# One more four-slot tile with seven-product pairs, a new written order, and early queries loaded in 2 KB runs

## The chip, the cores and the metric

The kernel runs on one core of a Trainium2 chip. TensorE (PE) does the matmuls, VectorE (DVE), ScalarE (ACT) and GpSimd (POOL) the elementwise work, and SyncE (SP) issues most DMAs. The metric is device time in microseconds; a lower one is better. Three runs of the kernel before gave 218.16, 218.23 and 218.40 us. The profiled execution that all rows come from has a span of 216.57 us from its first to its last instruction.

## The reference

Inputs are q, k and v of 4 batches, 8 heads, 768 tokens and 64 values a head, and three weights. First a retention with a decay per head, written as a recurrence:

```
state = gamma[h] * state + outer(k[t], v[t])
y[t]  = (1 / 8) * q[t] @ state
```

Then y, 3072 tokens by 512, goes through a bilinear feed-forward block of width 1536: `out = ((x @ w_a) * (x @ w_b)) @ w_out`. Outputs are float32; the kernel multiplies in bf16 and adds in float32.

## The kernel before

The 3072 tokens are 24 **slots** of 128, six to a batch. The recurrence is done in slots: q and k are scaled by powers of the decay (`scaled`, L281), so that within a slot the attention is a masked product of scores (`scores`, L366) with the values (`intra`, L415), and across slots a state of 64 x 64 a head is carried (`update`, L381) and multiplied by q (`inter`, L403). `leave` (L424) copies the finished y, transposed, to bf16 as the feed-forward input xt. Before that, q and k must be turned: `flip` (L330) does it with a transposing DMA on SP's queue.

Batch 0 is special, since nothing else can run until it is there. Its slots are handled in three pairs: one DMA loads 256 tokens of k, q or v with 2 tokens x 64 values (512 B) in a run (`load_two`, L135), partition p holding tokens 2p and 2p+1. `casts2` (L459) scales, `flip2` (L469) transposes on PE, and `scores2`, `update2`, `inter2`, `intra2` and `leave2` (L481 to L536) do the rest. The exponents for the scaling are made on the chip by `tables` (L196): an iota on POOL, a product on DVE, an exponential on ACT; the masks are memsets and selects on POOL (L219, L222), and `late_tables` (L229) makes a second set of tables for the other batches. `warm` (L549) puts idle matmuls on PE while it waits.

The slots are grouped in **tiles** for the feed-forward block: `TILES = [4, 2, 2, 2, 2, 4, 8]` (L16). The two stages of the block are tiled differently:

- First stage. For a plain tile, `ffn_a` (L560) and `ffn_g` (L574) multiply one block of 128 of the 1536 columns of w_a and of w_b with the whole tile as moving operand (256 or 512 columns, four matmuls each). ACT copies the first product to bf16, DVE multiplies the second with it. There are 12 such blocks. The tile of eight slots and, in part, the last tile of four (slots 12 to 15) use Strassen's scheme in Winograd's form instead: seven products of half size for eight, from sums of weight blocks (`weight_piece`, L807) and sums of inputs (`x_sum`, L827; `xf_sum`). For the eight-slot tile these are the classes `Unit` (L840, moving operand 512 columns); for the four-slot tile `Quad` (moving operand 256), for two pairs of blocks, p = 0 and 1, each pair and each weight on its own.
- Second stage. For all tiles but the first, a `Group` (L663) of seven products of 6 matmuls x 256 columns makes the outputs of two slots, from sums of the first stage (`hsum`, L642) and of w_out (`weight_sum`, L622). The first tile uses plain products (`ffn_out`, L599).

The order of work on every engine is the order of the program's text: `seq` chains each instruction to the one ahead of it on its engine. Up to the last block of tile 0 the text is a straight list. Behind it, calls such as `blocks(3, 6, 7)`, `turn(12, 10)` (L434: update, scores of the new pair, inter, intra and copy of the old pair, in one block), `hsums` and `casts(14)` stand in an order written by hand, with three strings for the laced stretches (`START`, `END`, `LACED`). `casts` also issues the loads of later slots. PE's accumulators are eight banks: three in a ring ("ff"), two for scores, two for y, one for the state.

Of the kernel before, what the change touches and what calls it, by code (L numbers as in the profile page):

```python
# [15 lines left out]
TILES = [4, 2, 2, 2, 2, 4, 8]  # L16
# [3 lines left out]
START = ("A1 A2 u0.1 u1.1 A6 T X3 A7 B1 X2 A5 B6 B7 X1 A3 B5 u0.2 u1.2 B2 X4 A4 u0.6 B3 u1.6 B4 u0.5 u1.5 "  # L20
         "u0.7 u2.1 u0.3 u1.7 u2.6 u1.3 u0.4 u2.2 u3.1 u2.5 u1.4 u2.7 u3.6")
END = ("u11.1 u10.5 u10.7 u9.4 u11.6 u10.3 u11.2 S03 a1< u11.5 u11.7 u10.4 b1< u11.3 a1> b1> c1< d1< u11.4 a7 c1> d1> c2 d2 "
       "S02 S01 b7 a2 b2 S04 a6 b6 S13 a5 b5 S12 a3 b3 a4 b4 S11 c7 d7 c6 d6 S14 c5 d5 "
       "c3 c4 d4 d3")
V_LATE = range(12, 20)
LACED = ("X3 X2 m1 m7 m2 a1 b1 a2 b2 m6 X1 a6 b6 a7 b7 F2 X4 m5 a5 b5 K20 G2 a3 b3 a4 b4 V18 "
         "m3 c1 d1 F3 H3 c2 d2 c6 d6 c7 d7 c5 d5 m4 c3 d3 V19 c4 d4 G3")
# [4 lines left out]
def kernel(  # L32
# [78 lines left out]

    def raw_tile(shape, dtype, tag, name):
        return raw.tile(shape, dtype, tag=tag, name=name, bufs=3 if tag == "vf" else 2)
# [3 lines left out]
    def load_slot(t, names="kqv"):  # L117
        b, ci = divmod(t, NCH)
        for nm in names:
            src = {"k": k, "q": q, "v": v}[nm]  # L120
            if nm == "q":
                if t % 2 == 0:
                    load_two(nm, src, b, ci // 2, t)
                continue
            if t % 2 == 0:
                whole[nm] = raw_tile([P, 2, H, D], F32, nm + "f", nm + "f")
            raws[nm, t] = whole[nm][:, t % 2]
            s = src[b, :, ci * P : (ci + 1) * P, :].rearrange("h p d -> p h d")
            seq(nc.sync.dma_start(out=raws[nm, t], in_=s))

    def load_slots(t):
        for u, names in ((t, "kq"), (t + 1, "k"), (t, "v"), (t + 1, "v")):
            load_slot(u, names)
# [8 lines left out]
    def load_pair(u):  # L142
        for nm, src in (("k", k), ("q", q), ("v", v)):
            load_two(nm, src, 0, u, 2 * u)
# [25 lines left out]
    def issue_loads(n):  # L170
        for _ in range(min(n, len(pending))):
            what = pending.pop(0)
            n = int(what[1:])
            if what[0] in "ab":
                load_wide(what[0], n)
            elif what[0] in "kqv":
                load_two(what[0], {"k": k, "q": q, "v": v}[what[0]], 0, n, 2 * n)
            else:
                {"p": load_pair, "s": load_slots, "t": load_slot, "w": load_w, "o": load_o}[what[0]](n)


    kqb = {}
# [11 lines left out]
    tabs = []  # L194

    def tables(pattern, channel):  # L196
# [8 lines left out]
        if not tabs:  # L205
            qtab = const.tile([P, NCH, H, 1], F32, name="qtab")
            seq(nc.scalar.activation(qtab[:, :, :, 0], earg, AF.Exp, bias=bq))
            tabs.append(qtab)
        tabs.append(ktab)

    tables([[2 * P, PAIRS], [1, 2], [0, 1]], 2)
    make_identity(nc, ident)
# [4 lines left out]
    for par in range(2):  # L217
        m = const.tile([P, 1, P], BF16, name=f"mask{par}")
        seq(nc.gpsimd.memset(m, 1.0))  # L219
        for c in range(2):  # L220
            mc = m[64 * c : 64 * c + 64]
            seq(nc.gpsimd.affine_select(out=mc, in_=mc, compare_op=ALU.is_ge, fill=0.0,  # L222
                                        base=-par, pattern=[[0, 1], [1, 2], [2, 64]],
# [5 lines left out]
    def late_tables():  # L229
# [3 lines left out]
        tables([[P, NCH], [0, 1]], 1)  # L233

# [32 lines left out]
    def cast_o(j):  # L267
        cast(nc.gpsimd, wo_bf[:, j * FPO : (j + 1) * FPO, :], wst["o", j])
# [12 lines left out]
    def scaled(eng, t, i):  # L281
        tab = tabs[0] if i else tabs[1 if t < 2 * PAIRS else 2]
# [5 lines left out]
        else:  # L288
            dst = dst.rearrange("p hp r d -> p r hp d")
# [3 lines left out]

    def new_nat(t):
        kqb[t] = nat.tile([P, 2, HP, 2, D], BF16, tag="kqb", name="kqb")
        kb[t], qb[t] = kqb[t][:, 0], kqb[t][:, 1]
        vb[t] = nat.tile([P, H, D], BF16, tag="vb", name="vb")

    def casts(t, between=lambda: None):
        new_nat(t)  # L300
        scaled(nc.gpsimd, t, 0)
        between()
        scaled(nc.gpsimd, t, 1)
        if t not in range(12, 20):
            cast(nc.gpsimd, vb[t], raws["v", t])
        u = t + 2
        if u == 20:
            load_slot(u, "kq")
        flip(t)
        if u == 20:  # L310
            load_slot(u + 1, "k")
            return
        if u == 21:
            load_slot(u - 1, "v")
            load_slot(u, "v")
            load_slot(22, "kq")
            return
        if u in V_LATE:
            if u == 13:
                load_slot(12, "q")  # L320
            elif u == 19:
                load_slot(18, "kq")
            load_slot(u, {12: "k", 18: ""}.get(u, "kq"))
            if u % 2:
                load_slot(u - 1, "v")
                load_slot(u, "v")
        elif u < NSLOT:
            load_slot(u)

    def flip(t):  # L330
        if t % 2 == 0:
# [4 lines left out]

    def late_kq(t):
        for u in (t, t + 1):
            new_nat(u)
            scaled(nc.gpsimd, u, 0)  # L340
            scaled(nc.gpsimd, u, 1)
            flip(u)
        if t == 20:
            load_slot(23, "k")
            load_slot(22, "v")
            load_slot(23, "v")

    def casts_two(t):
        for u in (t, t + 1):
            new_nat(u)  # L350
# [52 lines left out]
    def inter(t):  # L403
        if t % NCH == 0:
            return
# [863 lines left out]
```

## Time and profile before

| | |
|---|---|
| median of three runs | 218.23 us |
| profiled execution, span | 216.57 us |
| granted TensorE clock, mean | 1.000 |
| ACT busy | 104.9 us |
| POOL busy | 154.2 us |
| DVE busy | 147.5 us |
| DMA | 39.68 MB, 85162 packets |

A row of the timeline view reads: start, time until the last of the merged instructions ends, engine, line, operation, what is written from what, the part of PE's array in use (rows by columns), partitions by elements and type, how often; in brackets the idle time of the engine just before, and what ended it. Several equal instructions in sequence are merged into one row, and matmuls are pipelined, so the next row can start ahead of the end of the one before. In the windows view each engine has its busy time and its count, and the last three numbers are the granted clock, the DMA share and GB/s. DMA rows give the packets, their sizes and the mean rate of a stretch.

### The profile page before, as it was taken

To read this page: it belongs to the slowest core of one execution; us is meant where nothing else is said; L and a number is where in the kernel's file an instruction comes from. 1 tells how busy PE (TensorE), PEld (TensorE's weight loads), DVE (VectorE), ACT (ScalarE), POOL (GpSimd) and SP (SyncE) were. 2 spreads that over 40 slices of the span, in tenths; PEclk is the share of its full clock that TensorE was granted. 3 is DMA by queue.
4 is the path that set the end of the run, shared out by engine and by line. 5 is a ranking of instruction groups with operands and counts; after the bars stand their busy time and mean duration, and the time that the engine had idled before them with its cause. 6 is when DMAs were issued, how large, how long until landed. Compare 5 with 4: busy or idle time off the path is not lost.

```text
span 216.6 us, 5713 instructions
## 1 busy us (share of the span) xinstructions
PE 210.7 (97%) x2252; PEld 146.1 (67%) x2252; DVE 147.5 (68%) x272; ACT 104.9 (48%) x235; POOL 154.2 (71%) x184
## 2 busy tenths in 40 slices
PE   7889999999999999999999999999999999999994
PEld 3557445587458888888888877457864444458883
DVE  3777346845984486356377978676577987688962
ACT  3256325343224444464576475657546656652331
POOL 5265876879878678969869979899986999530000
PEclk9999999999999999999999999999999999999999
DMA  5999999999999999999979999950013000000055
GB/s 162 290 320 365 387 311 360 384 268 232 221 264 227 228 231 222 158 192 269 197 169 245 222 209 234 236 127 3 5 69 125 2 0 3 2 0 0 27 194 170
DMA packets 85162, 39.68 MB, mean 183 GB/s; under 512 B 57488, under 2 KB 78864, under 8 KB 85136
## 3 DMA queue, kind: packets, MB, share of 16 engines
q1 hardware_dynamic: 84992, 39.26, 76.8%
q8 instruction: 17, 0.28, 0.5%
q14 instruction: 9, 0.07, 0.1%
q10 hardware_dynamic: 144, 0.07, 0.1%
HBM read 28.31 MB, written 6.29 MB: 160 GB/s over the span
## 4 chain that ended last, share of the span: by engine, by line
PE 91%; SPq 3%; DMA 3%; POOL 0%; issue 0%; DVE 0%
PE a L568 18%; PE g L580 18%; PE mA L685 12%; PE uA L859 10%; PE mB L685 6%; PE o L605 5%; PE uB L859 5%; SPq L138 3%; DMA wsta<-in_moe_w_a_dram 3%; PE mC L685 3%; PE at L372 2%; PE uC L859 2%; PE y L420 2%; PE st L390 2%; PE fa L949 2%; PE fb L949 1%
## 5 line engine op out<-in xcount | busy, mean ns | idle before, releaser
L582 DVE TENSOR_TENSOR ht<-g,asb 128x256 bf16<-128x256 f32 (+1 forms) x70 | 34.4, 493 | 31.6 <-PE g L580 28.0
L568 PE MATMUL a<-xt,wa_bf 128*128 128x256 bf16 (+1 forms) x280 | 48.6, 300 | 0.1
L580 PE MATMUL g<-xt,wb_bf 128*128 128x256 bf16 (+1 forms) x280 | 48.4, 300 | 0.0
L571 ACT CAST asb<-a 128x256 bf16<-128x256 f32 (+1 forms) x70 | 30.0, 429 | 33.3 <-PE a L568 31.1
L580 PEld LDWEIGHTS <-wb_bf 128*128 128x128 bf16 x280 | 27.0, 98 | 10.2 <-POOL wb_bf L251 0.2
L568 PEld LDWEIGHTS <-wa_bf 128*128 128x128 bf16 x280 | 26.5, 98 | 10.7 <-POOL wa_bf L251 0.4
L292 POOL TENSOR_TENSOR kqb<-kf,ktab 128x512 bf16<-128x512 f32 x22 | 23.6, 1078 | 7.4 <-DMA kf<-in_k_dram 4.9
L866 ACT COPY snap<-uA 128x512 f32<-128x512 f32 x36 | 20.0, 588 | 15.4 <-PE uA L859 13.9
L685 PEld LDWEIGHTS <-hs 128*128 128x128 bf16 x234 | 22.8, 98 | 3.6
L378 DVE TENSOR_TENSOR aT<-at,mask 128x512 bf16<-128x512 f32 x36 | 22.3, 682 | 0.3
L292 POOL TENSOR_TENSOR kqb<-qf,qtab 128x512 bf16<-128x512 f32 x18 | 19.6, 1088 | 2.7 <-DMA qf<-in_q_dram 2.7
L618 POOL TENSOR_TENSOR ht<-gsb,asb 128x512 bf16<-128x512 bf16 x13 | 15.2, 1175 | 7.5 <-DVE gsb L618 7.4
L692 ACT COPY snaps<-mA 128x256 f32<-128x256 f32 x30 | 11.0, 374 | 18.9 <-PE mA L685 18.9
L685 PEld LDWEIGHTS <-ht 128*128 128x128 bf16 x180 | 17.5, 98 | 3.3
L618 POOL TENSOR_TENSOR hs<-ht 128x384 bf16<-128x384 bf16 (+3 forms) x14 | 15.9, 1134 | 3.5 <-DVE ht L582 3.5
L618 POOL TENSOR_TENSOR hs<-ht,hs 128x384 bf16<-128x384 bf16 (+1 forms) x17 | 16.9, 997 | 1.5 <-DVE ht L582 1.4
L685 PE MATMUL mA<-wsum,hs 128*128 128x256 bf16 x120 | 15.2, 273 | 0.0
L618 DVE TENSOR_TENSOR osb<-mB,snaps 128x256 f32<-128x256 f32 x20 | 8.4, 421 | 8.3 <-ACT snaps L692 4.4
L251 POOL CAST vb<-vf 128x512 bf16<-128x512 f32 x12 | 7.5, 641 | 6.7 <-DMA vf<-in_v_dram 6.7
L605 PE MATMUL o<-wo_bf,ht 128*128 128x512 bf16 x48 | 10.7, 379 | 0.0
L618 DVE TENSOR_TENSOR asb<-uB,snap 128x512 bf16<-128x512 f32 x12 | 8.2, 685 | 3.1 <-ACT snap L866 2.0
L618 DVE TENSOR_TENSOR gsb<-uB,snap 128x512 bf16<-128x512 f32 x12 | 8.2, 686 | 2.9 <-ACT snap L866 2.1
(138 smaller groups left out, 374.7 us busy)
## 6 DMA issues: line engine op xcount, KB each, us to landing
qf<-in_q_dram SPq DMA_DIRECT2D x12, 512.0 KB, 6.1
out_dram<-osb SPq DMA_DIRECT2D x21, 256.0 KB, 4.1
kf<-in_k_dram SPq DMA_DIRECT2D x18, 256.0 KB, 5.1
vf<-in_v_dram SPq DMA_DIRECT2D x18, 256.0 KB, 5.3
wsta<-in_moe_w_a_dram SPq DMA_DIRECT2D x6, 512.0 KB, 7.7
wsto<-in_moe_w_out_dram SPq DMA_DIRECT2D x6, 512.0 KB, 8.7
wstb<-in_moe_w_b_dram SPq DMA_DIRECT2D x5, 512.0 KB, 8.3
kf<-in_k_dram SPq DMA_DIRECT2D x3, 512.0 KB, 7.1
```

The costliest lines, as they stand in the source:

```text
L292: seq(eng.tensor_tensor(dst, src, tab, op=ALU.mult))
L378: seq(nc.vector.tensor_tensor(aT[t][:, r], at[r], mask.to_broadcast([P, HP, P]), op=ALU.mult))
L568: seq(nc.tensor.matmul(a, wa_bf[:, kt, fs], xcols(J, kt, c0, c1), start=(kt == 0), stop=(kt == KT - 1)))
L571: seq(nc.scalar.copy(asb, a))
L580: seq(nc.tensor.matmul(g, wb_bf[:, kt, fs], xcols(J, kt, c0, c1), start=(kt == 0), stop=(kt == KT - 1)))
L582: seq(nc.vector.tensor_tensor(ht[J][:, ft, c0:c1], g, asbs.pop((J, ft, c0)), op=ALU.mult))
L605: seq(nc.tensor.matmul(o, ht[J][:, ft, i * P : (i + 1) * P], wo_bf[:, ft], start=(ft == 0), stop=(ft == NFT - 1), skip_group_check=True))
L618: seq(eng.tensor_tensor(dst, x, y, op=op))
L685: seq(nc.tensor.matmul(m, w, right[:, j], start=(first and j == 0), stop=(j == NP - 1), skip_group_check=True))
L692: seq(nc.scalar.copy(self.snaps[:, n], self.bank["A"]))
L859: seq(nc.tensor.matmul(m, w, right[:, k], start=(first and k == 0), stop=(k == 1), skip_group_check=True))
L866: seq(nc.scalar.copy(self.snaps[n], self.bank["A"]))
```

## The change

Three things are changed.

1. `TILES` becomes `[4, 2, 2, 4, 4, 8]`: slots 8 to 11 are one tile. Both middle four-slot tiles (now numbers 3 and 4) use seven products for eight in the pairs p = 0 and 1. A class `Duo` replaces `Quad`: it takes both weights of a pair together, w_a in the left half of a bank and w_b in the right half, so that one ACT copy or one DVE sum treats 512 columns and the product of the two halves follows from that.
2. The hand-written calls and strings are replaced by one string `ORDER` of small steps, each with its engine where there is a choice (D, G and A for DVE, POOL and ACT). `turn` is gone: updates (U), scores (S), inter (I), intra (N) and copies (L) are steps of their own. Scalings of k and q (k, y), value casts (v), casts of w_out (C), sums (h, w, W, x, X), loads (l), flips (f) and stores (s) are steps too. On ACT a scaling is eight instructions, one a head.
3. For batch 0, q is loaded by two DMAs a pair, in runs of 8 tokens x 64 values (2 KB). A partition then holds one group of 8 tokens of one pair of heads. The queries come out of the transposition in another order, so `scores2` and `inter2` read them with a step of four values (`queries2`), masks and `leave2` follow that order, and a table of its own (`qtab2`) with the position and decay of each partition is made at the start. The usual q table is made later, in `late_tables`.

```
-TILES = [4, 2, 2, 2, 2, 4, 8]
+TILES = [4, 2, 2, 4, 4, 8]
+DUO = {3: {0: ('F', 'b', 'F', 'DGG', 'KKT'), 1: ('F', 'Z', 'F', 'DGG', 'OTO')}, 4: {0: ('F', 'b', 'F', 'DGG', 'KKT'), 1: ('F', 'Z', 'F', 'DGG', 'OTO')}}
+ORDER = """
+a.1.0 w.a.3.0.2.G C.4.G s w.a.2.0.2.D s C.3.G a.1.1 C.0.G C.2.G s a.1.2 w.b.3.0.2.D g.1.1 s C.5.G g.1.0 s
...
+w.b.2.0.2.D s a.1.5 g.1.10 g.1.4 g.1.9 g.1.5 s v.6.G y.6.G k.6.A s a.1.11 g.1.8 y.7.A f.6 k.8.G f.7
+g.1.11 s o.0.0 l.k.9 s W.3.D o.2.0 o.2.1 U.6.D l.v.9 o.0.1 l.k.10 W.2.D y.8.G f.8 W.1.D W.4.D l.v.10
+o.1.0 S.6.at.2 s S.7.y.2 v.7.G s o.1.1 h.1.3.0.6.D o.3.0 k.9.A h.1.2.0.6.D l.q.10 s v.10.G s o.3.1
...
+a.2.11 g.2.11 h.2.2.3.6.G h.2.1.3.6.G y.13.G h.2.4.3.6.G M.2.0.1 l.k.15 M.2.0.7 x.3.3.D y.14.G d.3.0.1
+x.3.2.D v.12.G d.3.0.7 x.3.1.D f.13 s M.2.0.6 d.3.0.2 M.2.0.2 d.3.0.6 d.3.1.1 a.3.2 x.3.4.D M.2.0.5
...
+    def load_pair_q(u):
+        f = raw_tile([P, 2, 8 * D], F32, "qf", "qf")
+        s = q[0, :, 2 * u * P : 2 * (u + 1) * P, :].rearrange("(hp r) (n j) d -> r n hp (j d)", r=2, j=8)
+        for r in range(2):
+            seq(nc.sync.dma_start(out=f[:, r], in_=s[r]))
...
     tables([[2 * P, PAIRS], [1, 2], [0, 1]], 2)
+    pick = osbp.tile([P, 3, HP, 32], F32, tag="osb", name="pick")
+    seq(nc.vector.tensor_copy(pick[:, :2], lgr.rearrange("p o (i r) -> p r i o", r=2).to_broadcast([P, 2, HP, 32])))
+    seq(nc.gpsimd.iota(pick[:, 2], pattern=[[0, HP], [8, 32]], base=0, channel_multiplier=0,
+                       allow_small_or_imprecise_dtypes=True))
+    posq = const.tile([P, PAIRS, 1, 8], F32, name="posq")
+    seq(nc.gpsimd.iota(posq, pattern=[[2 * P, PAIRS], [0, 1], [1, 8]], base=-MID,
+                       channel_multiplier=0, allow_small_or_imprecise_dtypes=True))
+    seq(nc.gpsimd.affine_select(out=pick, in_=pick, compare_op=ALU.is_equal, fill=0.0, base=0,
+                                pattern=[[0, 3], [-1, HP], [-4, 32]], channel_multiplier=1))
+    lgp = const.tile([P, 1, 3, 1], F32, name="lgp")
+    seq(nc.vector.tensor_reduce(lgp[:, 0, :, 0], pick.rearrange("p a i n -> p a (i n)"),
+                                axis=mybir.AxisListType.X, op=ALU.add))
...
+    seq(nc.scalar.activation(qtab2[:, :, :, :, 0], argq, AF.Exp, bias=bq))
     make_identity(nc, ident)
...
+            if eng is nc.scalar:
+                for h in range(H):
+                    seq(nc.scalar.mul(dst[:, h % HP, h // HP, :], src[:, h, :], tab[:, h, :]))
+                return
...
+    def queries2(u, rows, hp, c):
+        cols = kqT2[u].rearrange("p a b c (n i) -> p a b c i n", i=HP)
+        return cols[rows, :, 1, :, hp, 16 * c : 16 * c + 16]
...
-                                         kqT2[u][half(r), :, 1, hp, half(c)],
+                                         queries2(u, half(r), hp, c),
...
-            cast(eng, xt[J][:, i : i + 2, :, half(c)],
-                 ys[u][c].rearrange("p k (two n) -> p two k n", two=2))
+            cast(eng, xt[J][:, i + c].rearrange("p k (n j) -> p k n j", j=8),
+                 ys[u][c].rearrange("p k (j n) -> p k n j", j=8))
```

In `ORDER`, a and g are the two products of a plain block (tile, block), d a step of a `Duo` (tile, pair, product), M a step of a `Group` (tile, group, product), u a step of a `Unit`, o half of a plain output.

More of the change, by code (lines that the diff above doesn't have):

```diff
@@ L415, in intra @@
     def intra(t):
+        need(("S", t), ("v", t))
+        done.add(("N", t))
+        y_banks(t)
         for r in range(2):
@@ L575, in ffn_g @@
         c1 = TILES[J] * P if c1 is None else c1
+        done.update(("h", J, ft, c) for c in range(2))
         fs = slice(ft * P, (ft + 1) * P)
@@ L1242 @@
+    for step in ORDER.split():
+        kind, *args = step.split(".")
+        STEPS[kind](*args)
 _INS = ['q', 'k', 'v', 'moe_w_a', 'moe_w_b', 'moe_w_out']
```

675 lines of the change are left out of this document (295 added, 380 removed).

## The prediction

> **What bounds the kernel now.** The front page comes first, for who is busy; then the windows view in two stretches, cut where the first four-slot tile is through its feed-forward block; then PE's timeline, to see whether a busy PE is ever kept waiting.
>
> ```profile
> span 216.6 us, 5713 instructions
> PE 210.7 (97%) x2252; PEld 146.1 (67%) x2252; DVE 147.5 (68%) x272; ACT 104.9 (48%) x235; POOL 154.2 (71%) x184
> ```
>
> ```profile
> 0.00:42.00 42.00, 39.23 (x450) 22.32 (x450) 26.11 (x54) 17.89 (x35) 26.57 (x50) 1.00 1.05 320
> 42.00:216.60 174.60, 171.47 (x1803) 123.78 (x1802) 121.39 (x219) 87.01 (x200) 127.61 (x135) 1.00 0.71 150
> ```
>
> PE is busy for 171.47 us of the last 174.60, at clock 1.00, and no other engine reaches 75% there. Busy is not yet full speed, so the price of one matmul is read from starts:
>
> ```profile
> 42.51 0.60 PE L580 MATMUL g<-xt,wb_bf 128*128 128x256 bf16 x4
> 43.05 0.60 PE L568 MATMUL a<-xt,wa_bf 128*128 128x256 bf16 x4
> ...
> 112.06 0.60 PE L580 MATMUL g<-xt,wb_bf 128*128 128x256 bf16 x4
> 112.49 0.60 PE L568 MATMUL a<-xt,wa_bf 128*128 128x256 bf16 x4
> 113.01 0.60 PE L580 MATMUL g<-xt,wb_bf 128*128 128x256 bf16 x4
> 113.56 0.60 PE L568 MATMUL a<-xt,wa_bf 128*128 128x256 bf16 x4
> ...
> 138.20 1.03 PE L568 MATMUL a<-xt,wa_bf 128*128 128x512 bf16 x4
> 139.06 1.03 PE L580 MATMUL g<-xt,wb_bf 128*128 128x512 bf16 x4
> ```
>
> From 112.06 to 112.49 four matmuls of 256 columns take 0.436 us, 0.109 each; from 138.20 to 139.06 four of 512 take 0.864, 0.216 each. A step longer than that is a wait. Between feed-forward matmuls behind 42 us I find only four above 0.05 us, the first at 43.05 (0.11 over), the last at 113.56 (0.11 over), 0.38 together. So the kernel is PE's own list of matmuls, behind a start that ends near 18 us and ahead of a short tail.
>
> One thing in the list is not columns:
>
> ```profile
> 56.76 3.83 PE L605 MATMUL o<-wo_bf,ht 128*128 128x512 bf16 x17
> 60.52 0.32 PE L390 MATMUL st<-vb,kqb 128*64 128x64 bf16 x8
> ...
> 150.78 0.71 PE L685 MATMUL mA<-wsum,hs 128*128 128x256 bf16 x5
> 151.42 0.42 PE L410 MATMUL y<-kqT,gst 64*64 64x128 bf16 x16
> 151.77 0.64 PE L420 MATMUL y<-aT,vb 128*64 128x128 bf16 x16
> 152.34 0.83 PE L685 MATMUL mB<-wsum,hs 128*128 128x256 bf16 x6
> ```
>
> The number pair ahead of the tile size is the part of the array in use. When it changes, about 0.095 us pass: 17 x 0.216 = 3.67 from 56.76, and the next start is 0.09 later; 5 x 0.109 = 0.545 from 150.78, and the next is 0.095 later. Behind 42 us I count 39 such changes, the first at 60.52, the last at 152.34.
>
> **Columns.** Slots 8 to 11 are now two tiles of 256 columns: 12 blocks x 2 weights x 4 matmuls x 2 tiles = 192 x 0.109 = 20.93 us. Afterwards 8 blocks x 2 x 4 = 64 matmuls of 512 columns (13.82 us), and two pairs x 7 products x 2 weights x 2 = 56 of 256 (6.10): 19.93. That is **-1.00 us**, on PE and so on the path. Slots 12 to 15 have 56 and 64 such matmuls before and after: nothing. The second stage has ten groups of seven products in both: nothing.
>
> **Changes of the array's part.** Walking the written order from its first step to its last, with updates and intra products on one shape and scores and inter products on another, I count 48 changes against 39, because scores, updates and outputs of a pair no longer stand in one turn. 9 x 0.095 = **+0.86 us**. Every change of the trace pays it, so I allow 0.7 to 0.9.
>
> **Other engines.** The pairs give DVE, ACT and POOL other shapes of the same work. Key and query scalings, value and weight casts move between POOL, ACT and DVE, and with POOL at 127.61 of 174.60 us there is room. I cost this at nothing: it lies under PE's 171 us. If that cover fails at one hand-off, the price is the late result's own duration. The four visible waits (0.38 us) may go and others of their kind may come, for the sums of the four-slot tile are wanted soon after its last copy; I take 0, from -0.38 to +0.4.
>
> **The start.** Until 18.19 us PE runs a chain, and the early q and its tables touch it.
>
> ```profile
> 1.18 0.21 POOL L219 MEMSET mask<- 128x128 bf16 x1
> ...
> 3.54 0.30 POOL L231 TENSOR_SCALAR_AFFINE_SELECT mask<-mask 128x128 bf16<-128x128 bf16 x1
> 3.79 0.17 POOL L198 IOTA posp<- 128x6 f32 x1
> ```
>
> ```profile
> 0.98 0.48 DVE L186 MEMSET zero<- 128x512 f32 x1 [0.98 <-PEq L1253]
> ...
> 1.70 0.24 DVE L201 TENSOR_TENSOR earg<-posp,lgr 128x48 f32<-128x48 f32 x1
> ...
> 3.99 0.21 DVE L201 TENSOR_TENSOR earg<-posp,lgr 128x48 f32<-128x48 f32 x1 [1.50 <-POOL posp L198]
> 5.04 1.29 DVE L292 TENSOR_TENSOR kqb<-kf,ktab 128x512 bf16<-128x512 f32 x2 [0.84 <-DMA kf<-in_k_dram]
> 6.84 1.29 DVE L292 TENSOR_TENSOR kqb<-qf,qtab 128x512 bf16<-128x512 f32 x2 [0.51 <-DMA qf<-in_q_dram]
> ...
> 9.56 2.48 DVE L493 TENSOR_TENSOR aT<-at,mask 128x512 bf16<-128x512 f32 x4 [0.51 <-PE at L487]
> 12.21 1.50 DVE L292 TENSOR_TENSOR kqb<-qf,qtab 128x512 bf16<-128x512 f32 x2 [0.17 <-DMA qf<-in_q_dram]
> ```
>
> ```profile
> 9.10 0.64 PE L487 MATMUL at<-kqT 64*64 64x128 bf16 x32
> ...
> 15.21 0.64 PE L487 MATMUL at<-kqT 64*64 64x128 bf16 x32
> ...
> 18.19 0.42 PE L531 MATMUL y<-aT,vb 64*64 64x128 bf16 x16
> ```
>
> What it gives: the scaling of q waits for the load of q (0.51 and 0.17 us). Two loads give the rate by packet size, 5 to 14 us (packets of 512 B, a few of 1 KB) and 22 to 27 us (2 KB):
>
> ```profile
> DMA packets 4986, 2.64 MB, mean 293 GB/s; under 512 B 80, under 2 KB 4986, under 8 KB 4986
> ```
>
> ```profile
> DMA packets 994, 1.94 MB, mean 388 GB/s; under 512 B 55, under 2 KB 55, under 8 KB 993
> ```
>
> 524 KB take 1.79 us at 293 GB/s and 1.35 at 388, so the first q lands 0.44 us earlier, what follows the second 0.88. Each early q becomes two DMAs on SP's queue:
>
> ```profile
> 1.32 0.56 SPq L138 DMA_DIRECT2D qf<-in_q_dram  x1
> ```
>
> One issue more, some 0.5 us, puts v's from near 2 to near 2.5, while the data ahead of it are still moving at 5; I cost it at nothing. The Trainium skill, "DMA: Bandwidth & Descriptors", Specifications, says that line rate needs transfers of at least 512 B, by which q would gain nothing and this term would be 0. The two rows disagree: the measurement decides.
>
> What it takes: on POOL two iotas and a select over 384 values stand ahead of the masks, and that select waits for DVE's copy of 256 values, which stands behind the first exponents (1.70 + 0.24). By the memset of 512 values (0.48) the copy ends near 2.2. The select lies between one such select (0.30) and three (0.90): 0.7, so it ends at 2.9. From the first mask's memset to the DVE operation on the second iota are 3.99 - 1.18 = 2.81 us now, so that operation moves from 3.99 to about 5.7 (5.2 to 5.9). Queued behind it on DVE is the scaling of k, which moves from 5.04 to 5.95, and 1.29 us later q can follow, at 7.2 instead of 6.84 although q lies there since 6.4. Scores, masks and the second pair follow in a chain: **+0.2 us** at 18.19, between -0.44 (the preparation is over by 5.04) and +0.45.
>
> The early queries are then read with a step of four values; no row has that. If such a read costs double, scores (0.64 us for 32) and the inter products of three pairs cost some 1.5 us more. The Trainium skill, "SBUF — State Buffer", Door 1, says that a stride is free as long as 16 bytes are hit twice, up to 8 bf16 values; by it this costs nothing. No run here shows it yet. I take 0, the value of the contiguous rows, since the partition's bytes stay close together.
>
> **Sum.** -1.00 + 0.86 + 0 + 0.2 = +0.06 on the profiled span of 216.57, 216.63. The median of the runs, 218.23, lies 1.66 above that span, which I keep: **218.3 us**. The tail is unchanged.
>
> **Rivals.** A: columns against changes, the forecast; from 217.8 to 218.7.
>
> B: the start hides its preparation and no wait is left. For it: q's waits are visible, and POOL and DVE have idle time behind 4 us. Against it: DVE runs in order, and the late exponents stand ahead of k. -1.00 + 0.86 - 0.38 - 0.44 = -0.96: 217.3.
>
> C: slower, by the flips of slots 6 and 7. Now POOL scales them; afterwards k of 6 and q of 7 are eight ACT instructions each, and the transposing DMA of slot 7 waits for the last.
>
> ```profile
> 2.09 0.24 ACT L204 ACTIVATE ktab<-earg 128x48 f32<-128x48 f32 x1
> 2.24 0.32 ACT L207 ACTIVATE qtab<-earg,bq 128x48 f32<-128x48 f32 x1
> ...
> 50.67 0.37 ACT L571 CAST asb<-a 128x256 bf16<-128x256 f32 x1 [0.50 <-PE a L568]
> ```
>
> ```profile
> DMA to landing us min/median/max: 3.2/3.8/5.0
> ```
>
> ACT is free for them near 50: seventeen block steps of 0.436 behind 42.1, and that block's copy. One instruction of 64 values lies between 0.15 (from 2.09 to 2.24) and 0.37: sixteen and a copy end between 52.9 and 56.4, the transposition lands 3.2 to 5.0 later, between 56.1 and 61.4. PE reaches these scores at 59.4: 24 block steps (10.5), five output steps of 6 x 0.216 (6.5), an update and its changes (0.4). It decides from 0.32 us an instruction on (59.4 - 3.8 - 50.5 = 5.1 over 16). Its worst is 2.0 us, its middle 1.1: 219.4. For it: copies that free PE's banks queue behind the same sixteen. Against it: 64 values are nearer to 48 than to 256.
>
> D: the strided queries cost their 1.5 us: 219.8. For it speaks no row; its chance is small.
>
> **How the numbers follow.** A 0.42, B 0.36, C 0.16, D 0.06. A fifth of a per cent, 0.44 us, is about what a measurement of this kernel can tell. B is faster; A is the same but for 0.02 on its upper side; C and D are slower: 0.36, 0.40, 0.24. The range reaches from a little below B, 217.1, to C's middle and a little more, 219.7.
>
> **What would show it.** Right: 109 and 216 ns a matmul behind 42 us; 64 and 56 matmuls for slots 8 to 11; 48 changes at 0.095 us; k's first scaling near 5.95 and intra products at 18.4 instead of 18.19. Wrong: k still at 5.04 and scores by 8.7 (B); a PE gap of a microsecond ahead of the scores of slots 6 and 7 (C), or at any hand-off that I costed at nothing; 32 early scores above 0.64 us (D).

## The result: 224.8 us, 2.9% slower, and where the time went

The changed kernel takes 224.76 us (median of four runs, 223.70 to 225.25), the kernel before 218.24 us beside it. The ratio is 1.029, with a 95% interval from 1.027 to 1.032: the change costs 6.5 us. The forecast was 218.3 us, with a range from 217.1 to 219.7. A run over 1.5% above the fastest of its kernel counts as slow and is left out of its kernel's ratio; in the experiments these are one run each of E3, E10 and E11 and three of E8, which leaves E8 without a ratio, and the profiled runs of E3, E8 and E11 are among them. The profiled run of the changed kernel took 225.25 us. Its page opens:

```profile
span 223.5 us, 5530 instructions
...
PE 213.6 (96%) x2180; PEld 140.0 (63%) x2180; DVE 160.0 (72%) x285; ACT 108.8 (49%) x248; POOL 131.4 (59%) x158
```

PE still looks full, and POOL has 23 us less to do than before (154.2). The windows view, cut where the first block behind tile 0 starts (44.64 us now; that block started at 42.06 before), has for each engine the busy time and the count, then the granted clock, the DMA share and GB/s:

```profile
0.00:44.64 44.64, 41.07 (x450) 24.08 (x451) 27.33 (x58) 18.14 (x36) 27.89 (x53) 1.00 1.03 329
44.64:223.50 178.86, 172.51 (x1731) 115.90 (x1730) 132.68 (x227) 90.67 (x212) 103.49 (x107) 1.00 0.66 140
```

So 2.6 us are lost ahead of that block, and the rest takes 178.9 us where it took 174.5: another 4.4. PE has fewer matmuls there than before (1731 records for 1803) and 6.4 us in which it is not busy, where it had 3.1.

**The start.** The rows to compare with stood at 9.10, 15.21, 17.64 and 18.19 in the kernel before. This is the one at 17.64:

```profile
17.64 0.62 PE L520 MATMUL y<-kqT,gbd 128*128 128x128 bf16 x8
```

PE's timeline of the first two pairs now, with the four rows in the same order:

```profile
9.73 1.08 PE L546 MATMUL at<-kqT 64*64 64x128 bf16 x32
...
16.49 1.08 PE L546 MATMUL at<-kqT 64*64 64x128 bf16 x32
...
19.07 1.06 PE L579 MATMUL y<-kqT,gbd 128*128 128x128 bf16 x8
20.07 0.42 PE L590 MATMUL y<-aT,vb 64*64 64x128 bf16 x16
```

32 scores take 1.08 us where they took 0.64, and eight inter products 1.06 where they took 0.62. These are the matmuls that read the queries with a step of four values. What stands ahead of them on DVE:

```profile
5.79 1.29 DVE L392 TENSOR_TENSOR kqb<-kf,ktab 128x512 bf16<-128x512 f32 x2
7.47 1.29 DVE L374 TENSOR_TENSOR kqb<-qf,qtab 128x512 bf16<-128x512 f32 x2 [0.39 <-DMA qf<-in_q_dram]
```

k's scaling moved from 5.04 to 5.79, for the table work in front of it, and q's, at 7.47 instead of 6.84, still waits for its load: the second of the two DMAs lands at 7.34, where the one DMA before had landed at 6.75. Between PE's first scores and the first block behind tile 0 lie 34.91 us, where 32.95 lay before: of the 2.6 us, 0.63 are lost ahead of the scores and 1.96 behind them.

**The body.** PE's price of a matmul is what it was. From 91.73 to 92.59 four matmuls of 512 columns take 0.86 us:

```profile
91.73 1.03 PE L629 MATMUL a<-xt,wa_bf 128*128 128x512 bf16 x4
92.59 0.82 PE L743 MATMUL mA<-wsum,hs 128*128 128x256 bf16 x6
```

The part of the array in use changes 48 times. What is new is waits. The waits view of PE for 44.64 to 150 us (total, times, longest) and two of its places in the timeline, the wait in brackets:

```profile
PE mA L743 <- POOL hs L681: 0.9, 1, 0.9
PE at L434 <- DMA kqT<-kqb: 0.7, 2, 0.4
PE fA L992 <- ACT snapf L1005: 0.7, 1, 0.7
PE mA L743 <- DVE aT L440: 0.5, 1, 0.5
```

```profile
119.71 0.39 PE L743 MATMUL mA<-wsum,hs 128*128 128x256 bf16 x2 [0.91 <-POOL hs L681]
120.43 0.64 PE L434 MATMUL at<-kqT 64*64 64x128 bf16 x32 [0.33 <-DMA kqT<-kqb]
```

Summed over starts that come later than the matmul ahead of them allows, PE waits 4.9 us behind 44.64, where it waited 0.5 behind 42.06. The reasons named are all different engines, so the view is asked once more, for what POOL waits for; first the changed kernel from 44.64 to 150 us, then the kernel before from 42 to 150:

```profile
POOL kqb L392 <- DMA qf<-in_q_dram: 12.9, 4, 7.9
POOL vb L336 <- DMA vf<-in_v_dram: 11.6, 1, 11.6
POOL kqb L392 <- DMA kf<-in_k_dram: 8.7, 5, 4.2
```

```profile
POOL kqb L292 <- DMA kf<-in_k_dram: 3.6, 5, 1.6
POOL kqb L292 <- DMA qf<-in_q_dram: 2.7, 4, 1.4
```

POOL waits for loads for 33 us, where it waited for 6. It works in order, so the sums that PE wants at 119.71 stand behind a scaling of slot 18 that could begin only at 116.20, after 7.9 us of waiting for its load. And here is what the prediction did not look at, the DMA share by stage instead of as one mean. Windows of the kernel before, then of the changed one:

```profile
50.00:60.00 10.00, 10.00 (x61) 5.70 (x60) 8.35 (x12) 2.46 (x6) 8.64 (x9) 1.00 1.08 232
...
100.00:110.00 10.00, 10.00 (x95) 8.78 (x92) 3.86 (x10) 4.84 (x13) 8.09 (x9) 1.00 1.14 207
...
150.00:216.00 66.00, 63.49 (x446) 40.52 (x444) 48.56 (x79) 32.28 (x67) 36.16 (x37) 1.00 0.14 49
```

```profile
50.00:60.00 10.00, 10.00 (x79) 6.85 (x77) 5.05 (x11) 6.39 (x23) 5.49 (x7) 1.00 0.75 160
...
100.00:110.00 10.00, 9.62 (x141) 5.08 (x140) 8.07 (x15) 4.18 (x9) 8.26 (x9) 1.00 0.88 193
...
140.00:150.00 10.00, 10.00 (x183) 5.79 (x180) 8.62 (x14) 5.90 (x13) 5.78 (x7) 1.00 0.69 143
```

In the kernel before the DMA engines are full from 5 us to 140 (a share of 0.96 to 1.27 in the windows there; it passes 1 where the times of packets overlap) and nearly idle behind 150. The 0.71 that the prediction quoted for 42 to 216.6 us is the mean of these two stages. The changed kernel lets them idle for a part of 50 to 60 and of 100 to 110, and has more left to move behind 140 (0.69 for 0.48). The DMA view for 42 to 142 us, before and then after:

```profile
DMA packets 66523, 22.42 MB, mean 224 GB/s; under 512 B 55510, under 2 KB 64726, under 8 KB 66508
...
kqT<-kqb SPq DMA_TRANSPOSE x18, 4.7
```

```profile
DMA packets 65313, 21.48 MB, mean 215 GB/s; under 512 B 54648, under 2 KB 63864, under 8 KB 65299
...
kqT<-kqb SPq DMA_TRANSPOSE x17, 4.4
```

The last number of the second row is the median from issue to landing of a transposing DMA, a "flip". Five in six packets are under 512 B (the loads of k and v have runs of 256 B), and 215 to 224 GB/s come through in the mean, against 388 in 2 KB packets. The Trainium skill, "DMA: Bandwidth & Descriptors", Specifications, puts the least transfer for line rate at 512 B; for these packets the two rows agree with it.

### The profile page after: what moved, and what is told of

Read it like the earlier page. It is cut to its first block, busy times and chain, and to the rows that moved or that the text cites. A ratio compares the mean times of both kernels' runs of the same rounds, so it can differ in the third digit from the quotient of the medians.

```text
span 223.5 us, 5530 instructions
## 1 busy us (share of the span) xinstructions
PE 213.6 (96%) x2180; PEld 140.0 (63%) x2180; DVE 160.0 (72%) x285; ACT 108.8 (49%) x248; POOL 131.4 (59%) x158
## 4 chain that ended last, share of the span: by engine, by line
PE 82%; DMA 7%; DVE 4%; issue 2%; POOL 1%; SPq 1%; ACT 1%; POOLq 0%; DVEq 0%; ACTq 0%
PE a L629 14%; PE g L642 13%; PE mA L743 10%; PE uA L893 9%; PE mB L743 6%; DMA qf<-in_q_dram 5%; PE o L665 5%; PE uB L893 5%; PE fA L992 2%; PE mC L743 2%; PE uC L893 2%; PE at L434 2%; PE y L496 2%; DMA kqT<-kqb 2%; PE at L546 1%
## 5 line engine op out<-in xcount | busy, mean ns | idle before, releaser
L644 DVE TENSOR_TENSOR ht<-g,asb 128x256 bf16<-128x256 f32 (+1 forms) x54 | 28.9, 550 | 20.5 <-PE g L642 17.6
L629 PE MATMUL a<-xt,wa_bf 128*128 128x256 bf16 (+1 forms) x216 | 41.1, 324 | 0.1
L642 PE MATMUL g<-xt,wb_bf 128*128 128x256 bf16 (+1 forms) x216 | 40.3, 324 | 0.1
L642 PEld LDWEIGHTS <-wb_bf 128*128 128x128 bf16 x216 | 20.8, 98 | 12.6 <-issue 0.5
L629 PEld LDWEIGHTS <-wa_bf 128*128 128x128 bf16 x216 | 20.2, 98 | 12.0 <-DVE xt L336 0.3
L392 POOL TENSOR_TENSOR kqb<-kf,ktab 128x512 bf16<-128x512 f32 x17 | 18.2, 1073 | 9.9 <-DMA kf<-in_k_dram 9.9
L681 POOL TENSOR_TENSOR hs<-ht,hs 128x512 bf16<-128x512 bf16 (+1 forms) x9 | 10.0, 1114 | 8.0 <-DVE hs L681 7.9
L509 ACT CAST xt<-y 128x512 bf16<-128x512 f32 x18 | 9.7, 594 | 4.5 <-PE y L496 4.5
L1005 ACT COPY snapf<-fA 128x512 f32<-128x512 f32 x12 | 6.9, 586 | 8.9 <-PE fA L992 5.5
L681 DVE TENSOR_TENSOR hs<-ht,hs 128x1536 bf16<-128x1536 bf16 (+4 forms) x11 | 8.6, 777 | 3.4 <-POOL hs L681 3.3
```

The source lines that it names most:

```text
L392: seq(eng.tensor_tensor(dst, src, tab, op=ALU.mult))
L629: seq(nc.tensor.matmul(a, wa_bf[:, kt, fs], xcols(J, kt, c0, c1), start=(kt == 0), stop=(kt == KT - 1)))
L642: seq(nc.tensor.matmul(g, wb_bf[:, kt, fs], xcols(J, kt, c0, c1), start=(kt == 0), stop=(kt == KT - 1)))
L644: seq(nc.vector.tensor_tensor(ht[J][:, ft, c0:c1], g, asbs.pop((J, ft, c0)), op=ALU.mult))
L681: seq(eng.tensor_tensor(dst, x, y, op=op))
```

## The experiments

Two theories stood at first: the start is late for the early q alone, and the body is late because loads and flips reach POOL and PE late (with the rival that POOL, DVE and ACT hand over too late by themselves). In the table, "block" is the start of the first block behind tile 0, "rest" the span behind it, and the rate is that of the DMA engines from 42 to 142 us. These three come from one profiled run each.

| kernel | us (median, from to) | ratio (95%) | block | rest | GB/s |
|---|---|---|---|---|---|
| before | 218.23 (218.16 to 218.40) | | 42.06 | 174.5 | 224 |
| changed | 224.76 (223.70 to 225.25) | 1.029 (1.027 to 1.032) | 44.64 | 178.9 | 215 |
| E1 early q alone | 220.85 (220.49 to 221.67) | 1.013 (1.011 to 1.015) | 44.18 | 174.6 | 215 |
| E2 without early q | 225.74 (223.81 to 226.09) | 1.032 (1.028 to 1.037) | 42.09 | 182.1 | 219 |
| E3 queries side by side | 225.03 (222.60 to 226.07) | 1.027 (1.021 to 1.033) | 43.23 | 181.1 | 214 |
| E4 two loads sooner | 226.03 (224.02 to 227.32) | 1.035 (1.029 to 1.041) | 45.39 | 179.3 | 213 |
| E5 loads out | 221.09 (220.67 to 221.27) | 1.013 (1.011 to 1.014) | 44.18 | 175.3 | 109 |
| E6 loads unread | 225.85 (225.17 to 226.65) | 1.034 (1.031 to 1.038) | 44.33 | 180.2 | 215 |
| E7 E2, loads out | 218.90 (218.83 to 219.08) | 1.003 (1.002 to 1.004) | 41.96 | 175.1 | 120 |
| E8 E2, loads first | 237.15 (232.78 to 237.88) | | 42.10 | 193.6 | 207 |
| E9 E2, loads on ACT | 237.85 (236.07 to 237.95) | 1.088 (1.084 to 1.092) | 42.06 | 194.2 | 206 |
| E10 E2, loads on POOL | 247.46 (244.27 to 251.08) | 1.129 (1.121 to 1.136) | 42.11 | 203.5 | 178 |
| E11 E2, order mended | 226.55 (224.55 to 227.96) | 1.035 (1.030 to 1.040) | 42.02 | 184.2 | 216 |
| E12 before, more DMA | 231.50 (229.10 to 232.35) | 1.059 (1.051 to 1.067) | 42.01 | 187.6 | 212 |
| E13 E2, v out | 220.28 (219.29 to 220.77) | 1.009 (1.006 to 1.012) | 42.14 | 176.9 | 193 |
| E14 scalings on POOL | 223.82 (223.08 to 224.40) | 1.026 (1.023 to 1.028) | 44.17 | 177.2 | 217 |

**E1, the early q alone.** The kernel before with the third change only, its loads, tables, reads, masks and copies of the early q:

```
+            load_pair_q(u) if src is None else load_two(nm, src, 0, u, 2 * u)
...
+                                         queries2(u, half(r), hp, c),
```

> The kernel before with the early q alone (2 KB runs, its tables, the stepped queries); tiles and order as before. Theory 1 (the start costs on its own: first q later, tables on DVE ahead of k, stepped reads at double time): the first block behind tile 0 starts 2.1 us later, and nothing gives it back: 220.3 us. Theory 2 (the start only seems late because the new order changes what runs beside it): 218.2 to 218.6.

The block starts 2.1 us late and the rest takes as long as before, so this part costs 2.2 us by the spans (218.8 for 216.6) and 2.6 by the medians, and touches nothing behind the start. PE's first scores come 0.17 us late here, at 9.27, and from them to the block it is 34.91 us, as in the changed kernel.

**E2, all but the early q.** The reverse: the changed kernel with batch 0 loaded and read as before.

```
-            load_pair_q(u) if src is None else load_two(nm, src, 0, u, 2 * u)
+            load_two(nm, src, 0, u, 2 * u)
...
```

> The changed kernel with batch 0 loaded and read as before; tiles, pairs and order as changed. Theory 1 (start and order add up): 224.7 - 2.1 = 222.6 us, and PE's waits between 105 and 138 us are still about 4.8 us together. Theory 2 (the late start pushes the loads into those waits): the waits go too, 218 us.

The start is back at 42.09, and nothing is won: the rest takes 182.1 us. An earlier PE seems only to meet the flips earlier. The scores of the pair of slots 10 and 11 now wait, and the clock falls behind the wait. A row of PE's timeline and the windows of 80 to 90 us, whose clock is the third number from the end:

```profile
81.27 0.42 PE L402 MATMUL at<-kqT 64*64 64x128 bf16 x16 [1.78 <-DMA kqT<-kqb]
```

```profile
80.00:90.00 10.00, 8.73 (x125) 6.67 (x126) 6.15 (x10) 4.16 (x10) 8.14 (x9) 0.83 1.06 217
```

So the two costs do not add up: something other than PE paces the body.

**E3, queries side by side.** The copy behind PE's transposition puts the queries of a group next to each other, so that scores and inter products read them without a step; the rest of the change stays.

```
-            cast(eng, kqT2[u][:, pars[0] : pars[0] + len(pars), i], tp)
+            for n, par in enumerate(pars if i else ()):
+                cast(eng, kqT2[u][:, par, 1].rearrange("p j (i n) -> p j i n", i=HP),
+                     tp[:, n].rearrange("p j (n i) -> p j i n", i=HP))
...
```

> The changed kernel, where the copy out of the transposition puts the queries of one head pair side by side, so that scores and inter products read 16 neighbouring values. Theory 1 (a read with a step of four values runs at half speed): 32 early scores take 0.64 instead of 1.08 us, inter products 56 instead of 113 ns a matmul, and the time falls by about 1.6 us to 223.1. Theory 2 (they are slow for another reason, such as late weights): 224.7, and the 1.08 us stay.

```profile
15.76 0.64 PE L550 MATMUL at<-kqT 64*64 64x128 bf16 x32
...
17.90 0.62 PE L583 MATMUL y<-kqT,gbd 128*128 128x128 bf16 x8
```

The matmuls have their old duration again, which shows that the step was the cause. The block starts 1.4 us sooner than in the changed kernel, but the step costs more than that. From PE's first scores to the block it is 34.91 us in the changed kernel, E1, E5, E6 and E14, which all read with the step, and 32.95 before: 1.96 us for the step. Here it is 33.58, and most of the remaining 0.63 is a wait for this kernel's own copies:

```profile
37.58 0.64 PE L550 MATMUL at<-kqT 64*64 64x128 bf16 x32 [0.61 <-DVE kqT L336]
```

The later waits take the gain back, as in E2.

**E4, two loads sooner.** The loads of q and k of slot 18, for which POOL waited 7.9 us, stand right behind the flip of slot 14.

```
-f.15 d.3.0.4 f.14 d.3.1.4 g.3.3
+f.15 d.3.0.4 f.14 l.q.18 l.k.18 d.3.1.4 g.3.3
...
-L.12 l.k.18 a.3.4 g.3.4 s S.15.y.2 l.q.18 U.14.A
+L.12 a.3.4 g.3.4 s S.15.y.2 U.14.A
```

> The changed kernel with two loads (q of slots 18 and 19, k of 18) issued some 5 us sooner in SP's list, right behind the flip of slot 14; nothing else moves. Theory 1 (POOL runs in order and stands idle 7.9 us for this q, and the sums queued behind it come late to PE): PE's waits at 113 to 125 us, 2.6 us together, go, so 222.1 us, less if the later waits shrink too. Theory 2 (the waits belong to the pairs' own banks and copies): 224.7.

The wait at 119.7 us for POOL's sums goes, but the rest does not get shorter (179.3): PE waits 1.4 us at 121.4, for a flip, and 2.1 at 138.4, for ACT, which waits 3.3 us for a store to land, in its place. What one transfer gains, others lose here.

**E5, loads left out.** The loads of slots 10 to 23 are not issued; their scalings and casts read slots 8 and 9 again. This and the next three tell the loads from the hand-offs of the engines.

```
+        if t >= 10:
+            raws[nm, t] = raws[nm, 8 + t % 2]
+            return
```

> Leaves out: the loads of k, q and v of slots 10 to 23; their scalings and casts read the values of slots 8 and 9 again, so everything else (scalings, transposing DMAs, sums, matmuls, their order) stays as in the changed kernel. Theory L (the body's waits come from loads that land late: SP issues them in order behind the transposing DMAs, and POOL, which waits for them in order, holds up the sums behind it): PE's waits behind its first feed-forward block fall from 4.9 us to under 1, the stretch from that block to the last matmul to 171.2 (170.8 to 172.2), the start stays late by 2.1 to 2.6, together 220.4 us (219.8 to 221.4). Rival H (POOL, DVE and ACT hand over too late by themselves in the new order, whatever the loads do): at least 3 us of the waits stay, 223 us or more.

PE's longest wait behind the block is 0.6 us, and the rest takes 175.3 us: 3.6 of the 4.4 us are gone with the loads. The DMA view for 42 to 142 us:

```profile
DMA packets 30865, 10.90 MB, mean 109 GB/s; under 512 B 27396, under 2 KB 29444, under 8 KB 30851
...
kqT<-kqb SPq DMA_TRANSPOSE x18, 3.1
```

The flips land 3.1 us behind their issue instead of 4.4. The rival, late hand-offs without any load, falls: the engines do all else that they did.

**E6, loads that nobody waits for.** The loads are issued, but scalings and casts read one fixed block of four heads.

```
+            src = (src.rearrange("p (r hp) d -> p r hp d", r=2) if t < 10
+                   else same.to_broadcast([P, 2, HP, D]))
```

> Leaves out: the use of the loads of slots 10 to 23. They are issued and land as in the changed kernel, but scalings and casts read one fixed block of four heads in their place, so no engine waits for a load; SP's queue and the DMA engines have the same work. It tells two forms of theory L apart. If what counts is that the data land late: waits under 1 us and 220.4 us (219.8 to 221.4), as without the loads. If what counts is the time that SP and the DMA engines spend on them ahead of the transposing DMAs: waits of 2 us or more stay, 222 to 225 us. Rival H: 223 us or more.

It is no faster than the changed kernel. So it is not enough that nobody waits for the data; what counts is the time that the loads take on SP's queue and the DMA engines. SP's queue and PE's timeline show one case:

```profile
108.67 0.70 SPq L198 DMA_DIRECT2D qf<-in_q_dram  x1
...
113.15 2.62 SPq L420 DMA_TRANSPOSE kqT<-kqb  x1
```

```profile
119.48 0.64 PE L440 MATMUL at<-kqT 64*64 64x128 bf16 x32 [1.28 <-DMA kqT<-kqb]
```

The flip of slot 17 goes out at 113.15, behind four loads issued from 108.16 to 111.03, and lands at 119.43, 6.3 us later; the scores wait for it. In E5 the same flip, issued at 113.47 with no load ahead, lands 3.3 us later.

**E7, the same without the early q.** E2 with the loads of E5 left out.

> Leaves out the same loads as the first run of this call, from the changed kernel with batch 0 loaded and read as before the change (that one took 225.7 us with 7.9 us of waits, though its first feed-forward block started as early as before). Theory L: the block starts at 42.1, the rest takes 171.2 to 171.8 (columns -1.0, changes of the array's part +0.86), 218.2 us (217.8 to 219.0). Rival H: waits of 3 us or more stay, 221.5 us or more.

It takes 218.90 us, and the waits view of PE has one entry in the whole body, 0.2 us. From the block's start to the start of the last matmul it is 171.17 us, against 171.21 before, where the prediction's columns and changes say 0.14 less. The other 0.6 us stand at the very end: the last store lands at 215.54 (215.65 before), but 1.5 us pass from there to the end of the span instead of 0.9. No row says why. Without these loads the new order is therefore as good as the old one, and no better.

**E8, loads first.** E2 with each load right behind the step that frees its buffer.

```
-v.6.G y.6.G k.6.A s a.1.11 g.1.8 y.7.A f.6 k.8.G f.7
+v.6.G y.6.G l.v.9 l.v.10 l.v.11 k.6.A l.k.10 l.k.11 s a.1.11 g.1.8 y.7.A l.q.10 f.6 k.8.G f.7
...
```

> Changed kernel with batch 0 loaded and read as before the change; each load of slots 9 to 23 stands in the written order right behind the step that frees its buffer (the scaling or cast of the pair that had it), never later than it stood. All work is done. Theory L, where only the place of the loads is wrong: most of the 7.9 us of waits go, 218.0 to 220.0 us. If two or three buffers are too few, or the transposing DMAs now stand behind more loads and are late in their turn: 221 us or more, with waits of scores for the transposed keys and queries. Rival H: 222 us or more, with waits for sums.

This is the worst order of all on SP. The first flip goes out at 62.71 us instead of 53.62 in E2, and PE waits for flips four times:

```profile
57.44 2.37 SPq L187 DMA_DIRECT2D kf<-in_k_dram  x2
62.30 0.37 SPq L197 DMA_DIRECT2D qf<-in_q_dram  x1
62.71 1.99 SPq L381 DMA_TRANSPOSE kqT<-kqb  x1
```

```profile
PE at L401 <- DMA kqT<-kqb: 14.6, 4, 8.8
```

So the place of the loads is not simply "too late": loads and flips stand in each other's way.

**E9 and E10, loads on another queue.** E2 with the loads of slots 10 to 23 issued by ACT, and by POOL.

```
-        seq(nc.sync.dma_start(out=raws[nm, t], in_=s))
+        seq((nc.scalar if t >= 10 else nc.sync).dma_start(out=raws[nm, t], in_=s))
```

> Changed kernel with batch 0 as before the change (225.7 us), and the loads of slots 10 to 23 are issued by ACT in place of SP, at the same places of the written order (two loads of q stand a little later, behind the step that frees their buffer). All work is done. Theory Q (the transposing DMAs are late because they stand behind loads in SP's queue, in issue and in service): they land 3.1 to 3.6 us behind their issue again, as without loads, and most of the 7.9 us of waits go: 218.5 to 221 us, some of it for ACT's own 0.4 to 0.6 us an issue. Theory E (the two share the DMA engines, whatever queue they come from): they still take 4.3 us and more, and 223 us or more. Rival: ACT waits for free buffers and its copies hold up PE: new waits for ACT, 223 us or more.

> As the run before, but POOL issues the loads of slots 10 to 23; it does most of the scalings that free their buffers itself, so it waits for little. Theory Q: transposing DMAs at 3.1 to 3.6 us, waits under 2 us, 218.5 to 220.5 us. Theory E: they still take 4.3 us and more, 223 us or more. Rival: an issue costs POOL a microsecond or more of its own, its sums come late and PE waits for them, 221 us or more.

Both are far slower. With ACT, SP is free and issues a flip in 1.35 us on average instead of 2.07, but the flips still land 4.3 us later in the median, up to 8.7: they share the DMA engines with the loads, whatever queue these come from. The DMA view has the two queues (share of 16 engines last), and ACT's timeline what the issues do to ACT:

```profile
q1 hardware_dynamic: 27006, 10.16, 51.5%
q10 hardware_dynamic: 33320, 10.24, 51.4%
```

```profile
125.95 2.59 ACTq L188 DMA_DIRECT2D vf<-in_v_dram  x1
128.63 3.54 ACTq L188 DMA_DIRECT2D vf<-in_v_dram  x2
132.27 2.03 ACTq L198 DMA_DIRECT2D qf<-in_q_dram  x1
134.34 0.37 ACT L716 COPY snaps<-mA 128x256 f32<-128x256 f32 x1 [7.36 <-issue]
```

These four issues take from 1.1 to 2.6 us each (the second row merges two), and ACT's copy waits behind them. With POOL the flips take 5.6 us in the median and the rate falls to 178 GB/s. In both the theory of the shared engines held, together with the rival that the issuing engine is held up. A part of the time in E8 to E10 is PE's clock, which was at half for 10 to 21 us in each, behind such waits.

**E11, the order mended at seven places.** E2 with all its loads on SP; each step on these lines stands behind the first one of its line now.

```
+l.v.9 l.v.10
...
+f.8 l.k.10 l.k.11 l.q.10
...
+f.9 l.q.12
...
+y.13.G l.q.16
...
+y.17.G k.17.G f.17
...
+h.3.2.4.6.G y.18.G k.18.G
...
+y.19.G l.q.22
```

> Changed kernel with batch 0 as before the change (225.7 us), all loads on SP, all work done; only the written order is changed at the places where its trace shows waits: the loads of v and k of slots 10 and 11 and of q of 10 and 12 sooner, but none ahead of the transposing DMAs of slots 6 and 7; k of slot 17 scaled by POOL right behind q of 17, with its transposing DMA ahead of four loads; q and k of 18 scaled behind the sums that POOL owes PE at 120 us. Theory Q or E (lead of transposing DMAs and loads is what counts, and can be had by the order): waits fall from 7.9 us to 1 to 3, 219 to 221.5 us. If waits only move on to other places, as in the runs that mended one place: 223 us or more.

A miss. The waits that were meant go (the flip of slot 17 lands 4.8 us ahead of its scores), and 2.5 us for the flips of slots 10 and 11, 1.5 for an ACT copy that waits for a store, 1.2 and 1.1 others come.

**E12, more DMA time for the kernel before.** 14 loads of 128 KB that nothing reads.

```
+            if nm == "v" and t >= 10:
+                seq(nc.sync.dma_start(out=spare, in_=s[:, :HP]))
```

> The kernel before, with one more load of 128 KB (four heads of v again, in the same 256 B runs) behind each load of v of slots 10 to 23; nothing reads it. All of the computation is done. Theory E (the DMA engines are full from 20 to 140 us in the kernel before too, and it has no waits only because its loads and transposing DMAs just come in time): 14 loads of 128 KB at the 5.4 us a MB that the loads took (share of the DMA engines with and without them) are 10 us more of DMA time ahead of 140 us; waits of 3 us or more appear in a kernel that had 0.4, 221 to 228 us. Rival S (only the order of SP's queue in the changed kernel is bad; the DMA engines have room): under 1 us of waits, 218.2 to 219 us.

The order without waits has them now: 231.5 us, 13.3 more. The waits view of PE from 42 to 160 us, that of SP's queue from 42 to 140, and the DMA view from 42 to 142:

```profile
PE at L375 <- DMA kqT<-kqb: 6.1, 3, 3.8
PE mB L688 <- POOL hs L621: 1.0, 1, 1.0
PE mA L688 <- POOL hs L621: 0.9, 1, 0.9
```

```profile
SPq L131 <- DMA spare<-in_v_dram: 12.7, 4, 3.6
```

```profile
DMA packets 64034, 21.24 MB, mean 212 GB/s; under 512 B 54194, under 2 KB 62386, under 8 KB 64020
```

More is asked for and less comes through (212 GB/s for 224). Some 4 of the 13 us are PE's clock, at half behind two of the waits (121.6 to 125.0 and 148.9 to 155.7 us). The size of the loss fits DMA engines that are full in the kernel before too, with waits that its order only just avoids; it does not prove it. All 14 loads write one buffer, so the second of a pair waits on SP's queue until the first has landed, 12.7 us in all, and the flips behind it wait with it: PE's two longest waits, to 120.87 and to 150.4, are for flips that SP issued behind such waits, which ended at 114.0 and 141.2. How much of the 13 us is the fullness, and how much this wait, would take a second buffer to tell, which was not run.

**E13, a dose.** E2 without the loads of v of slots 10 to 23, a third of the bytes.

> Leaves out: the loads of v of slots 10 to 23 alone (their casts read v of slots 8 and 9 again), from the changed kernel with batch 0 as before the change, which took 225.7 us with all loads and 218.9 us without any. A third of the loads' bytes. Theory E: the DMA engines get some 19 us of 120 free, and most of the waits go: 219 to 221 us. Rival S: SP still issues the rest in the same places behind the same steps: 222.5 to 225 us.

220.28 us, between 225.74 with all and 218.90 with none. The DMA share of 60 to 140 us is 0.84, against 0.41 with no loads, and 5.5 of the 6.8 us between the two are back with a third of the bytes. The loss is not in proportion to the bytes, as one expects if it begins where the engines are full.

**E14, the scalings of ACT on POOL.** The changed kernel with four steps of the order renamed.

```
-k.6.A
+k.6.G
...
-y.7.A
+y.7.G
...
-k.9.A
+k.9.G
...
-y.10.A
+y.10.G
```

> The changed kernel whole, but the four scalings that ACT does in eight instructions each (k of 6 and 9, q of 7 and 10) are done by POOL at the same places of the order. All of the computation is done. Theory E with gaps: the transposing DMAs of slots 6 and 7 go out about 2 us sooner, the DMA engines' idle time between 50 and 60 us (share 0.75 where the kernel before has 1.08) closes, and what it cost later, some 1 to 3 us, comes back: 222 to 224 us. Rival: the waits behind 100 us have nothing to do with it, 224.5 us and more.

The DMA share of 50 to 60 us rises from 0.75 to 0.92, and the time falls by 0.9 us. The runs of the two kernels overlap (to 224.40, from 223.70), so this is a hint that part of the loss comes from flips that wait for ACT, with the loads behind them on SP; it is not more.

None of these kernels beats the kernel before, and E7 says why none was to be expected: PE's own list is no shorter.

## Why the prediction was wrong, point by point

- **Price of a matmul, columns, changes of the array's part:** right. 0.109 and 0.216 us stand, and 48 changes; with the loads out (E7) the body is 171.17 us, 0.04 less than before, where -1.00 + 0.86 = -0.14 was said.
- **"Other engines. ... I cost this at nothing: it lies under PE's 171 us":** this step failed, and with it "the four visible waits ... I take 0, from -0.38 to +0.4". It measured +4.4 us, of which 3.6 go when the loads are left out (E5). Busy time of POOL, DVE and ACT was asked for room, and it was there (POOL even lost 23 us of work); what had no room were the transfers, on the DMA engines and on SP's queue that feeds them. The prediction had 0.71 in its own fence and never split that stage. Split at 140 us it reads 0.96 to 1.27 and then 0.5 and less, and a new order of loads, scalings and flips can then delay what PE waits for, however idle the other engines are. Lead shows it too: in the kernel before the later flip of a pair lands 2.8 us or more ahead of its scores, in the changed kernel less than 0.1 us ahead for slots 14 and 17, for which PE stood waiting.
- **The start, +0.2:** this step held, and its size came out where no other delay fell on the run; most of the 2.6 us at the first block belong to the next point. k's scaling was put at 5.95 and came at 5.79. In E1, E5 and E14, which load batch 0 in the same way, q's scaling follows it at 7.01 (7.2 was said) and the first scores come 0.16 or 0.17 us late. In the profiled run of the changed kernel they come 0.63 late, since its second DMA of q landed at 7.34, where it landed from 6.68 to 6.83 in those three: a difference between runs that no step of the prediction is about. The gain of 0.44 us from 2 KB runs is in none of them, since the one DMA before had landed at 6.75. That the second issue takes up the gain is likely, but no run has one without the other. For the second pair 0.88 was hoped for; its last DMA lands at 12.29, in those three from 11.69 to 11.79, where it landed at 12.19.
- **Stepped reads, "I take 0":** this failed too, and it is the larger part of the start; it was the rival D at 0.06. It measured 0.44 us more for 32 scores and as much for eight inter products, together 1.96 us from the first scores to the block (D said some 1.5). E3 shows the step as the cause. The page that spoke for 0, the Trainium skill, "SBUF — State Buffer", Door 1, says that a step of up to 8 bf16 values is free; the trace disagrees for a step of 4.
- **Rival C** (flips of slots 6 and 7 late by ACT's sixteen scalings): PE did not wait at its place. But its first half happened, since ACT works on them until 57 us and SP holds the loads behind these flips: the DMA engines idle in 50 to 60 us. E14 puts the cost of that at 0.9 us, with runs that overlap.
- **Range and chances:** slower was given 0.24, by two mechanisms, one priced by ACT's time and one by PE's. No case let the transfers have no room, though the profile had the numbers for it.

What stays open: which waits appear in a given order, since they differ from run to run (kernels with the new order and all loads scatter by 1.3 to 6.8 us, the kernel before by 0.3); why this order delays the transfers more than the old one, beyond the hint of E14; whether the kernel before would bear a load more without waits; and the 0.6 us at the end of E7.

## What to carry to other kernels

Before an edit is costed at nothing because an engine has room, read the share of every resource by stage, the DMA engines first: a mean of 0.71 was 1.1 for more than half of the time and 0.14 at its end. Where transfers are full, a new order of work is a new order of transfers, and mending one wait moved it here (E4, E11); only leaving loads out helped (E5, E7, E13). To tell late data from busy transfers, leave the transfers out in one run and keep them unread in another, as E5 and E6 do. A run that adds load tells less when the load brings a wait of its own, as the one buffer of E12 does. And before a step is judged by when the next stage begins, measure from its own first instruction: the block's start mixed the 1.96 us of the stepped reads with a load that came late in one run.

## What the runs showed of the hardware that was not expected

- A moving operand read with a step of four bf16 values (8 bytes) makes a matmul slower: 32 of 128 columns in 1.08 us for 0.64.
- With full DMA engines a transposing DMA lands 4.3 to 5.6 us behind its issue in the median, and up to 8.7 with the loads on ACT's queue (E9) or 13.9 with them on POOL's (E10); with little beside it 3.1 (E5).
- With full DMA engines an issue can hold the issuing engine: up to 2.6 us for a load on ACT (E9), where 0.37 is the least.
- PE's clock fell to half behind a wait of 1.78 us in the midst of dense work (E2, from 82.3 to 85.7 us), which adds 1.7 us to the wait. The Trainium skill, "TensorE: Matmul & The Clock Gate", Part 1, gives an idle window of some 3.4 us for this; here the clock fell behind one of half that length. It did not do so behind each: it stayed at 1.00 behind 1.97 us in E4 and behind 2.77 us in E9.
